# A gather and scatter kernel that sorts edges first: shorter last chunks, chunks of 16 tiles with one-hots on GpSimd in the first stage, and fewer VectorE operations

## The chip, the cores and the metric

The kernel runs on one core of a Trainium2 chip. The core has TensorE (PE, matrix products; its weight loads are listed apart as PEld), VectorE (DVE), ScalarE (ACT), GpSimd (POOL) and SyncE (SP), and 16 DMA engines that all queues share. The metric is the device time of one execution in microseconds; lower is better. A profile is taken of one execution; its span runs from the first to the last instruction.

## The reference

There are N = 10000 nodes with features x of shape (N, 64, 4), and E = 640000 edges. Each edge has a source, a destination, a vector Y of 4 and a feature vector of 4. All is float32, and source and destination are drawn at random.

```python
R = silu(edge_feat @ w_rad)                    # (E, C)
xs = x[src]                                    # (E, C, M)
tp = einsum('eci,ef,ifo->eco', xs, Y, cg)      # (E, C, M)
msg = R[:, :, None] * tp
agg = segment_sum(msg.reshape(-1, C * M), dst, N).reshape(N, C, M)
return einsum('ncm,cd->ndm', agg, w_mix)
```

## The kernel before

The kernel never adds into memory edge by edge. It sorts the edges by destination, in two passes, so that the edges of 32 neighbouring nodes (a bucket) lie in one block of slots, and then sums each bucket with matrix products. Edges are handled in tiles of 128, one per partition; 5000 tiles in all. What is moved for an edge is a record of W = 9 words: source and destination packed into one word, Y, and the edge features.

**Parts.** `SPLIT` cuts the edges into three parts of 1488, 1776 and 1736 tiles. Pass 1 (`pass1`) distributes the records of a part over NG = 20 groups (array `grp` in DRAM); pass 2 (`pass2`) distributes a group's records over its 15 or 16 buckets (array `bkt`). A segment is one group of one part, so there are 60 segments. `messages` then works through the buckets in units of 5 tiles (first part) or 6 (the others): it gathers rows of x, one indirect DMA on GpSimd per tile (`gather`, line 808), multiplies them by the radial factors (`products`, line 852), builds S from one-hots and Y (`spots`, lines 842 and 845) and sums G on TensorE (`sums`, line 863). The sums of the first two parts go to DRAM and are added to in the next; the third part ends with the mix by `w_mix` and the store of the output (`mix`, line 911).

**Stages.** `run` has three. The lead-in is pass 1 of the first part alone. There only SP's order is written out by hand, and the other engines' is made by a scheduler. The second stage, `groups`, writes out the order on TensorE, VectorE and ScalarE: it interleaves the generators of `messages`, pass 2 of the next segment, and pass 1 of the next part, each by a count of steps that are due. The orders of GpSimd and SP are the scheduler's. The third stage, `overflow`, is a loop on the device over records that found no room, 128 slots an iteration; each iteration is a chain of a load, a gather of x, a gather of the output, products and a scatter to the output (lines 1062 to 1142).

**One chunk of a pass** (`route`). A chunk is up to T = 24 tiles of one part or segment (`even` splits evenly: 62, 74 and 73 chunks in pass 1, 4 in each segment of pass 2). `tables` has counted before, for up to `NC` chunks at a time, how many edges of each tile go to each of the B targets; `digits` makes the 0/1 array `D` that it counts. For a chunk, `places` and `placed` compute for every edge its position through two products and a copy on ScalarE; `slots` (lines 482 to 485: a maximum and three small operations on VectorE) turns it into a row (0 to 127) and a slot. `spread` builds X: a mask (line 496) and a product of mask and record (line 499), for 6 tiles at a time, as wide as the widest of the six needs. `onehots` builds `oh`, the one-hot of the rows: with 12 tiles in a piece (half a chunk), 6 are made by VectorE (line 512) and `act` = 6 by ScalarE (lines 517 and 518). `move` multiplies `oh` by X into PSUM (line 528), `evict` copies the result to `rt`, and `store` (line 546) writes its rows, each S slots long, with one indirect DMA on GpSimd. Steps are spread over the counter k of `route`: a chunk is loaded 6 steps ahead, its positions come 5 and 4 ahead, slots 3 ahead.

**Overflow of a chunk.** A target has a fixed room (`cap`). If a chunk's end for a target lies beyond it, the whole block of that chunk and target (R rows of S slots) goes to the overflow area instead (`over` and `inc`, lines 420 to 424; `ko`, lines 445 to 447), and the count in `kov`, in blocks, sets the number of iterations in `overflow` (line 1044). R is 6 in pass 1 and 8 in pass 2, S is 39 and 35.

The array `self.dv` in PSUM holds constants that VectorE reads (`v128`) and two scratch areas (`eq` of `spots`, `vmsk` of `spread`), so that an operation reads at most one operand from SBUF.

Of the kernel before, what the change touches and what calls it, by code (L numbers as in the profile page):

```python
# [60 lines left out]
class Pass:  # L61
# [18 lines left out]
    def spans(self, a, z):  # L80

        return [(t, min(t + 6, z), max(self.w[t:min(t + 6, z)])) for t in range(a, z, 6)]
# [19 lines left out]
class Kernel:  # L102
    def __init__(self, ctx, tc, x, src, dst, Y, ef, w_rad, cg, w_mix, out):
# [40 lines left out]
        self.p1 = Pass(T, NG, P // NG, [n / N for n in self.gn], 1.5, 5e-9)  # L144
# [6 lines left out]
        p, R = self.p1, self.p1.R  # L151
        self.gcap = [max(g) * P // R for g in self.gt]
        p.stride = [-(-(c + p.S) // 64) * 64 for c in self.gcap]
        p.base = [0]
        for st in p.stride:
            p.base.append(p.base[-1] + NG * R * st)
        p.ovf = p.base[-1]
        p.blocks = sum(len(even(z - a, T)) for a, z in self.part) * NG
# [3 lines left out]
        p.blocks = sum(len(even(t, T)) for t in sum(self.gt, [])) * MB  # L162
        for p in (self.p1, self.p2):
            p.slots = p.ovf + p.blocks * p.R * p.S + 2 * P
        self.p1.key, self.p2.key = "grp", "bkt"
        self.xw = max(sum((z - a) * w for a, z, w in p.spans(c, d)) * W for p in (self.p1, self.p2)
                      for m in range(T // 2, T + 1) for c, d in p.pieces(m))

        self.p1.NC, self.p2.NC = 12, max(len(even(t, T)) for t in sum(self.gt, []))
        self.p1.dst = self.dr.tile([self.p1.slots, W], F, name="grp")  # L170
        self.p2.dst = self.dr.tile([self.p2.slots, W], F, name="bkt")
# [3 lines left out]
        self.held, self.wanted, self.pos = None, False, None  # L175

# [6 lines left out]

    def consts(self):
        nc, c = self.nc, self.cst

        def iota(name, pat, base=0, cm=0, at=c):
            t = at.tile([P] + [n for _, n in pat], F, name=name)
            nc.gpsimd.iota(t, pattern=pat, base=base, channel_multiplier=cm,
                           allow_small_or_imprecise_dtypes=True)  # L190
            return t
# [11 lines left out]
        self.eq = self.dv[:, P:P + UT * NB].rearrange("p (t n) -> p t n", n=NB)  # L203
        self.vmsk = self.dv[:, P + UT * NB:]
# [9 lines left out]
        for p in (self.p1, self.p2):  # L214

            k, T, B = p.key, p.T, p.B
            p.cols = c.tile([64, B * (T + 1)], F, name="cols" + k)
            nc.vector.memset(p.cols, 0.0)
            nc.vector.memset(p.cols.rearrange("p (b t) -> p b t", b=B)[:, :, 0:1], RESET)
            p.low = c.tile([64, B * (T + 1)], F, name="low" + k)  # L220
            nc.gpsimd.memset(p.low, 0.0)
            p.lot = c.tile([P, T], F, name="lot" + k)
            nc.gpsimd.memset(p.lot, 0.0)
            for t in range(T):
                if p.lo[t]:
                    nc.gpsimd.memset(p.low.rearrange("p (b t) -> p b t", b=B)[:, :, t:t + 1], float(p.lo[t] * p.R))
                    nc.gpsimd.memset(p.lot[:, t:t + 1], float(p.lo[t]))
            p.A = c.tile([P, P], BF, name="A" + k)
            nc.vector.tensor_scalar(p.A, self.U, float(B), None, op0=OP.mult)
            nc.vector.scalar_tensor_tensor(p.A, self.ident, BIG, p.A, op0=OP.mult, op1=OP.add)  # L230

            j = iota("j" + k, [[0, 1]], base=0, cm=1, at=self.ph)
            ji = self.ph.tile([P, 1], I32, name="ji" + k)
# [220 lines left out]
    def route(self, ps, chunk, sizes, table):  # L454
# [97 lines left out]
        for k in range(-6, NP + self.ls):  # L552
# [20 lines left out]
            if k % 2 and 0 <= k + 3 < NP:  # L573
                slots((k + 3) // 2)
# [638 lines left out]
```

## Time and profile before

| | us |
|---|---|
| median of 3 runs | 8622.01 |
| lowest and highest run | 8620.0, 8624.1 |
| the profiled execution | 8610.05 |
| its span | 8608.1 |

| stretch of the span, us | what runs |
|---|---|
| 0 to 36 | constants, first loads, first tables |
| 36 to 588 | lead-in: pass 1 of the first part |
| 588 to 738 | pass 2 of the first segment, pass 1 of the second part beside it |
| 738 to 3195 | messages of the first part, by the gathers' issue |
| 3195 to 5875 | messages of the second part |
| 5875 to 8328 | messages of the third part |
| 8328 to 8608 | last sums and stores, then the overflow loop |

Over the whole span TensorE is busy 86% of the time, VectorE 81%, GpSimd 65% and ScalarE 43%. In a table of stretches each row has start and end, length, then for each engine the busy time and the number of instructions, the granted TensorE clock as a share of full speed, the busy share of the DMA engines and GB/s. A row of waits reads: engine and line that waited, what it waited for, total us, times, longest. A row of a timeline has the start, the length, the engine, the line, the operation with its tiles and shapes, and in brackets the idle time before it. A row of groups has line, engine, operation, shape and count, then busy time and the mean of one in ns. On GpSimd, 0.30 us between two indirect DMAs appears as idle time ("issue").

### The profile page before, as it was taken

Reading aid. Unit: us, or ns where it says so; the run is one execution under the profiler, and the core shown is the slowest. Engines: PE = TensorE matmul, PEld = TensorE weight load, DVE = VectorE, ACT = ScalarE, POOL = GpSimd, SP = SyncE. Lnnn points to the kernel's source line nnn. Section 1 sums busy time; section 2 is a strip of 40 time slices with the busy share of each in tenths; the row PEclk is TensorE's granted clock in tenths of the full one; section 3 lists DMA queues with packets and bytes.
Section 4 is the critical chain, followed back from the end, with each engine's and each line's share of the span. In section 5 each row is a group of like instructions: output and inputs, shape, how many; then the busy total and the mean of one; then the engine's idle time right before and its main releaser. Section 6 shows DMA issues by size and latency. Waiting matters only on the chain. (4 is left out here: it accounts for less than half of the span.)

```text
span 8608.1 us, 141721 instructions
## 1 busy us (share of the span) xinstructions
PE 7366.7 (86%) x49106; PEld 6316.5 (73%) x49106; DVE 6967.2 (81%) x13381; ACT 3692.0 (43%) x10312; POOL 5578.9 (65%) x5982
## 2 busy tenths in 40 slices
PE   7878989889989888999999899887988998889862
PEld 6767777777877777777777778766777777777651
DVE  8988888898988789999999999776776677667533
ACT  6765555555555444444444445332332233223200
POOL 0104766666666767777676777777777777777751
PEclk9988989899999899999989999988989999899875
DMA  7113444344444444545454554554444444444430
GB/s 271 46 30 86 136 117 118 112 122 119 122 119 120 134 121 139 142 139 145 135 140 136 143 144 135 156 145 138 134 134 133 136 134 133 134 135 131 132 91 11
DMA packets 677211, 1086.50 MB, mean 126 GB/s; under 512 B 255927, under 2 KB 481651, under 8 KB 670232
## 3 DMA queue, kind: packets, MB, share of 16 engines
q0 software_dynamic: 282384, 774.50, 31.7%
q1 hardware_dynamic: 392968, 295.28, 11.9%
q8 instruction: 389, 6.37, 0.3%
q10 hardware_dynamic: 1152, 7.74, 0.2%
q14 instruction: 318, 2.61, 0.1%
HBM read 857.68 MB, written 222.06 MB: 125 GB/s over the span
## 5 line engine op out<-in xcount | busy, mean ns | idle before, releaser
L808 POOL DMA_INDIRECT xg<-in_x_dram,sidx x5321 | 5072.6, 953 | 1976.3 <-issue 1406.1
L528 PE MATMUL pr<-X,oh 128*128 128x135 f32 (+14 forms) x20530 | 2754.9, 294 | 342.3 <-DVE oh L512 247.8
L528 PEld LDWEIGHTS pr<-X,oh 128*128 128x128 f32 x20530 | 2623.4, 202 | 507.9 <-DVE oh L512 281.7
L863 PE MATMUL G<-S,xg 128*128 128x128 f32 x21284 | 2933.0, 301 | 11.3 <-DVE Gs L892 5.2
L863 PEld LDWEIGHTS G<-S,xg 128*128 128x128 f32 x21284 | 2831.5, 216 | 71.1 <-DVE Gs L892 33.8
L852 DVE TENSOR_TENSOR xg<-xg,pre 128x1536 f32<-128x1536 f32 (+1 forms) x939 | 1558.4, 1660 | 864.1 <-DMA xg<-in_x_dram,sidx 717.6
L499 DVE TENSOR_TENSOR X<-dv,Wt 128x918 f32<-128x918 f32 (+12 forms) x1796 | 1620.5, 902 | 163.8 <-PE pr L528 82.2
L517 ACT ACTIVATE sq<-i,row 128x128 f32<-128x128 f32 x5388 | 1663.2, 390 | 47.8 <-DVE row L485 39.9
L834 ACT ACTIVATE pre<-pre 128x384 f32<-128x384 f32 (+1 forms) x939 | 429.8, 458 | 2172.4 <-PE pre L831 2102.3
L845 DVE TENSOR_TENSOR S<-dv,pay 128x768 f32<-128x768 f32 (+1 forms) x939 | 857.5, 913 | 53.6 <-PE G L863 9.4
L831 PE MATMUL pre<-wr,sT 54*128 54x384 f32 (+1 forms) x1878 | 836.7, 526 | 22.6 <-ACT sT L826 22.5
L518 ACT ACTIVATE oh<-sq,ones 128x768 f32<-128x768 f32 x898 | 838.4, 934 | 27.5 <-issue 1.7
L512 DVE TENSOR_TENSOR oh<-dv,row 128x768 f32<-128x768 f32 (+3 forms) x898 | 780.3, 873 | 0.2
L821 PEld LDWEIGHTS pre<-ident,pay 128*54 128x54 f32 (+1 forms) x939 | 108.8, 116 | 859.7 <-DVE xg L852 676.2
L821 PE MATMUL pre<-ident,pay 128*54 128x128 f32 (+1 forms) x939 | 293.5, 313 | 511.7 <-DVE xg L852 491.6
L546 POOL DMA_INDIRECT grp<-rt,idx x209 | 213.0, 1019 | 678.4 <-ACT rt L537 477.7
L826 ACT ACTIVATE sT<-pre 54x128 f32<-54x128 f32 (+1 forms) x939 | 246.5, 262 | 818.4 <-PE pre L821 816.1
L496 DVE TENSOR_TENSOR dv<-dv,slot 128x102 f32<-128x102 f32 (+12 forms) x1796 | 445.9, 248 | 40.3
L476 ACT ACTIVATE pc<-pp 128x480 f32<-128x480 f32 (+6 forms) x449 | 226.2, 504 | 410.5 <-DVE pos L482 282.5
L831 PEld LDWEIGHTS pre<-wr,sT 54*128 54x128 f32 (+1 forms) x1878 | 282.7, 188 | 151.8 <-issue 42.6
L842 DVE TENSOR_TENSOR dv<-dv,dlc 128x192 f32<-128x192 f32 (+1 forms) x939 | 331.2, 353 | 18.1
L911 PE MATMUL po<-wf,Gs 128*128 128x256 f32 (+1 forms) x1280 | 306.8, 394 | 38.5 <-DVE over L420 31.5
(210 smaller groups left out, 4098.7 us busy)
## 6 DMA issues: line engine op xcount, KB each, us to landing
xg<-in_x_dram,sidx POOLq DMA_INDIRECT x5321
sums<-Gp SPq DMA_DIRECT2D x626, 128.0 KB
old<-sums SPq DMA_DIRECT2D x626, 128.0 KB
bkt<-z SPq DMA_DIRECT2D x26, 1024.0 KB
grp<-z SPq DMA_DIRECT2D x16, 1024.0 KB
pay<-bkt SPq DMA_DIRECT2D x208, 54.0 KB
ys<-in_Y_dram SPq DMA_DIRECT2D x96, 96.0 KB
es<-in_edge_feat_dram SPq DMA_DIRECT2D x96, 96.0 KB
```

The lines of the kernel that those rows point to most:

```text
L496: nc.vector.tensor_tensor(msk, self.v128[:, :w].unsqueeze(1).to_broadcast([P, m, w]), slot[:, t:e].unsqueeze(2).to_broadcast([P, m, w]), o ...
L499: nc.vector.tensor_tensor(x, msk.unsqueeze(3).to_broadcast([P, m, w, W]), CH[c][1][:, t:e, :].unsqueeze(2).to_broadcast([P, m, w, W]), op= ...
L512: nc.vector.tensor_tensor(oh[:, :v, :], self.v128.unsqueeze(1).to_broadcast([P, v, P]), row[:, a:a + v].unsqueeze(2).to_broadcast([P, v, P ...
L517: nc.scalar.activation(sq[:, u - v, :], self.i128, AF.Square, bias=row[:, a + u:a + u + 1], scale=-1.0)
L518: nc.scalar.activation(oh[:, v:m, :], sq[:, :m - v, :], AF.Relu, bias=self.ones[:, 0:1], scale=-2.0)
L528: nc.tensor.matmul(PR[c][:, ps.lo[t] * W:ps.hi[t] * W], oh[:, u, :], Xs[u], start=(t == 0), stop=(t == sizes[c] - 1), skip_group_check=True)
L808: nc.gpsimd.indirect_dma_start(out=xg[:, t, :], out_offset=None, in_=self.x, in_offset=bass.IndirectOffsetOnAxis(ap=si[:, u:u + 1], axis=0))
L831: nc.tensor.matmul(R, ST_.pop(k)[:ut * W], self.wr[:ut * W, :ut * 64], start=True, stop=True)
L834: nc.scalar.activation(RT[k], RT[k], AF.Silu)
L845: nc.vector.tensor_tensor(S[:, :ut], self.eq[:, :ut].unsqueeze(3).to_broadcast([P, ut, NB, 4]), pb[:, :, 1:5].unsqueeze(2).to_broadcast([P ...
L852: nc.vector.tensor_tensor(V, V, R.unsqueeze(3).to_broadcast([P, ut, 64, 4]), op=OP.mult)
L863: nc.tensor.matmul(G[:, h].rearrange("p n f -> p (n f)"), V[:, t, 32 * h:32 * h + 32, :].rearrange("p c i -> p (c i)"), S[:, t].rearrange( ...
```

## The change

*Last chunk.* `sizes2` gives the segments of the third part a fifth chunk of 6 tiles; the other four share the rest (22, 22, 22, 21 and 6 where it was 24, 23, 23, 23). Rows of that chunk have S = 12 slots. The overflow counts slots now, not blocks: `over` is multiplied by a column `sc` of slots per block (one more VectorE operation in `tables`), and a row `ov` replaces the factor R x S.

*Lead-in.* Pass 1 of the first part has an own `Pass` with T = 16 (93 chunks, S = 28, pieces of 8 tiles) and tables for up to 18 chunks at a time. With `spare` set, which it is in the lead-in alone, all one-hots beyond `act` = 3 are single operations on GpSimd, one for each tile of 128 x 128: 930 in all. `rt` has 20 buffers for 16, and stores come 10 steps after, not 8.

*Mask and X.* `spread` makes one mask and one X for a whole piece, with the width of the piece's widest tile.

*Slots.* The maximum stays one for each chunk; the three operations after it are done for two chunks at once. For this, chunks are loaded 8 steps ahead, positions come 7 and 6 ahead, and slots 5 ahead.

*Digits.* `two` holds each digit twice in bf16, and the compare reads `ib` (bf16, SBUF) and `two` (bf16, SBUF) in place of `v128` (float32, PSUM) and the integer digits; one operation covers 38 tiles (pass 1) or 48 (pass 2), not 24.

```diff
+    def width(self, a, z):
+        return max(self.w[a:z])
...
+        early, late = some(16), some(T)
+        self.p1 = [early] + [late] * (len(SPLIT) - 1)
...
+    def sizes2(self, k, g):
+        n, T, end = self.gt[k][g], self.p2.T, 6 if k == len(SPLIT) - 1 else 0
+        return even(n - end, T) + [end] * (end > 0)
...
     def digits(self, ps, D, dig, nt):
-        for o in range(0, nt, 24):
-            m = min(24, nt - o)
-            self.nc.vector.tensor_tensor(D[:, o:o + m, :], self.v128[:, :ps.B].unsqueeze(1).to_broadcast([P, m, ps.B]),
-                                         dig[:, o:o + m].unsqueeze(2).to_broadcast([P, m, ps.B]), op=OP.is_equal)
+        nc, B, q = self.nc, ps.B, 768 // ps.B // 2 * 2
+        two = self.ph.tile([P, dig.shape[1], 2], BF, name="two", tag="two" + ps.key, bufs=1)
+        nc.vector.tensor_copy(two[:, :nt], dig[:, :nt].unsqueeze(2).to_broadcast([P, nt, 2]))
+        yield
+        for o in range(0, nt, q):
+            m = min(q, nt - o)
+            nc.vector.tensor_tensor(
+                D[:, o:o + m, :].rearrange("p t (b e) -> p t b e", e=2),
+                self.ib[:, :B].rearrange("p (b e) -> p b e", e=2).unsqueeze(1).to_broadcast([P, m, B // 2, 2]),
+                two[:, o:o + m].unsqueeze(2).to_broadcast([P, m, B // 2, 2]), op=OP.is_equal)
             yield
...
-        nc.vector.tensor_tensor(over[:N], e[:N], cap[:N], op=OP.is_gt)
-        nc.vector.tensor_tensor_scan(inc[:N], self.ones[:N, :B], over[:N], 0.0, op0=OP.mult, op1=OP.add)
+        nc.vector.tensor_tensor(over[:N, :B], e[:N], cap[:N], op=OP.is_gt)
+        nc.vector.tensor_scalar(over[:N, B:], over[:N, :B], sc[:N], None, op0=OP.mult)
+        nc.vector.tensor_tensor_scan(inc[:N], self.ones[:N, :B], over[:N, B:], 0.0, op0=OP.mult, op1=OP.add)
...
-        nc.vector.tensor_scalar(ko, Kp, float(R * ps.S), ps.ovj[:Q], op0=OP.mult, op1=OP.add)
+        nc.vector.tensor_tensor(ko, Kp, ov[:Q, :N], op=OP.add)
...
         def slots(c):
+            m, a = sizes[c], c % 2
...
+            nc.vector.tensor_reduce(pos[:, a, :m], PP.pop(c).rearrange("p (t b) -> p t b", b=B), axis=AX.X, op=OP.max)
+            if a == 0 and c + 1 < N:
+                return
...
         def spread(k):
-            for t, e, w in ps.spans(a, z):
-                m = e - t
...
+            m, w = z - a, ps.width(a, z)
+            msk = self.vmsk[:, :m * w].rearrange("p (t s) -> p t s", s=w)
+            nc.vector.tensor_tensor(msk, self.v128[:, :w].unsqueeze(1).to_broadcast([P, m, w]),
+                                    slot[:, a:z].unsqueeze(2).to_broadcast([P, m, w]), op=OP.is_equal)
...
+            nc.vector.tensor_tensor(X, msk.unsqueeze(3).to_broadcast([P, m, w, W]),
+                                    CH[c][1][:, a:z, :].unsqueeze(2).to_broadcast([P, m, w, W]), op=OP.mult)
...
         def onehots(k):
-            if v:
+            if self.spare:
+                for u in range(v):
+                    nc.gpsimd.tensor_scalar(oh[:, u, :], self.i128, row[:, a + u:a + u + 1], None, op0=OP.is_equal)
+            elif v:
...
-        for k in range(-6, NP + self.ls):
+        for k in range(-8, NP + self.ls):
...
-            self.rt_bufs, self.ls, self.act = 16, 8, 6
+            self.rt_bufs, self.ls, self.act, self.spare = 20, 10, 3, True
...
-                first = self.pass1(0, 4)
+                first = self.pass1(0, 6)
...
-            self.rt_bufs, self.ls, self.act = 3, 4, 6
+            self.rt_bufs, self.ls, self.act, self.spare = 3, 4, 6, False
```

More of the change, by code (lines that the diff above doesn't have):

```diff
@@ L184, in consts @@
     def consts(self):
         nc, c = self.nc, self.cst
[L187 to L191, printed above, removed]
+        iota = self.iota
         self.zr = c.tile([16, 8 * W], F, name="zr")
@@ L450, in tables @@
         nc.vector.tensor_tensor(idx[:Q, :N], ko, ii, op=OP.add)
-        self.tab[ps.key] = (sb, idx)
+        self.tab[ps.key] = (sb, idx, runs)
         yield
```

245 lines of the change are left out of this document (132 added, 113 removed).

## The prediction

> **What bounds the kernel now.** I read the table of time slices first, then cut the span where the work changes (first gather of x, last gather of each part of `SPLIT`, end of the messages) and read the busy time of each engine in each stretch.
>
> ```profile
> core 0: us, PE busy (x) PEld busy (x) DVE busy (x) ACT busy (x) POOL busy (x), PEclk, DMA share, GB/s
> 36.00:588.00 552.00, 470.43 (x3244) 406.99 (x3244) 523.14 (x1090) 408.66 (x1107) 61.43 (x62) 0.96 0.32 114
> 588.00:738.00 150.00, 102.97 (x604) 87.21 (x604) 118.00 (x299) 77.67 (x213) 9.93 (x11) 0.72 0.13 34
> 738.00:3195.00 2457.00, 2177.12 (x15013) 1897.40 (x15011) 2134.86 (x4248) 1305.91 (x3727) 1655.02 (x1723) 0.90 0.43 122
> 3195.00:5875.00 2680.00, 2397.38 (x16497) 2065.08 (x16498) 2397.41 (x4365) 1174.82 (x3234) 1940.41 (x2026) 0.92 0.51 142
> 5875.00:8328.00 2453.00, 2126.88 (x13488) 1802.22 (x13487) 1670.90 (x2828) 702.57 (x1950) 1858.44 (x1950) 0.90 0.47 133
> 8352.00:8608.00 256.00, 72.35 (x184) 44.74 (x184) 97.34 (x436) 13.26 (x56) 41.94 (x42) 0.50 0.05 11
> ```
>
> Five stretches, three limits. The lead-in (36 to 588 us) is VectorE's: 523 of 552 us busy, with GpSimd nearly idle. The messages of the third part (5875 to 8328) are GpSimd's. Its waits there are all one kind:
>
> ```profile
> POOL xg L808 <- issue: 512.1, 1681, 0.3
> POOL bkt L546 <- issue: 21.0, 69, 0.3
> ...
> PE pr L528 <- DVE oh L512: 83.7, 40, 5.4
> PE pre L821 <- DVE xg L852: 81.4, 54, 4.1
> ```
>
> No wait of POOL in that stretch is above 0.3 us, so 1950 indirect DMAs in 2453 us, 1.258 us each, is its full rate, though it shows as 76% busy. By that rate the messages of the first part need 1723 x 1.258 = 2168 of 2457 us and those of the second 2026 x 1.258 = 2549 of 2680: POOL has 289 and 131 us to spare there. VectorE is 87% and 89% busy in them, TensorE 89% each at a granted clock near 0.9, and the longest waits of TensorE (last two lines above, first part) are for VectorE. So these two are set mostly by VectorE, with GpSimd close behind. The last 256 us are the overflow loop (lines 1062 to 1142), one latency chain with every engine mostly idle.
>
> **The change part by part.**
>
> *The overflow loop.* A chunk's block that would pass a bucket's end goes whole to the overflow area, in R x S slots: 8 x 35 = 280 now. The loop takes 128 slots an iteration.
>
> ```profile
> 8403.99 1.01 POOL L1140 DMA_INDIRECT out_dram<-ocur,odi  x1 [8.19 <-DVE ocur L1139]
> ...
> 8580.02 1.01 POOL L1140 DMA_INDIRECT out_dram<-ocur,odi  x1 [8.24 <-DVE ocur L1139]
> ```
>
> In GpSimd's timeline these two end the 3rd and 13th iteration of 14: 176.03 / 10 = 17.60 us each. Applying the kernel's slot rules to the reference's edges with seed 0 gives 6 overflowing blocks, all last chunks of the third part: 6 x 280 = 1680 slots, 13.1, so 14 iterations, as the profile has. Afterwards the last chunk is 6 tiles, S = 12, 96 slots; the same rules give again 6 blocks, 576 slots, 4.5, so 5 iterations. 9 x 17.60 = **-158 us**. Nothing hides this loop, so nothing hides its loss. The lower count of slots is exact if the six blocks stay six; a seventh or eighth would cost at most one iteration.
>
> *The fifth chunk.* Each of 20 segments of the third part gets one more store on POOL, the engine that sets that stretch.
>
> ```profile
> 4309.16 0.95 POOL L808 DMA_INDIRECT xg<-in_x_dram,sidx  x1 [0.30 <-issue]
> 4310.41 1.51 POOL L808 DMA_INDIRECT xg<-in_x_dram,sidx  x1 [0.30 <-DVE Gp L892]
> 4332.28 1.02 POOL L546 DMA_INDIRECT grp<-rt,idx  x1 [0.30 <-issue]
> 4333.61 0.96 POOL L808 DMA_INDIRECT xg<-in_x_dram,sidx  x1 [0.30 <-issue]
> 4309.98 1.18 DVE L395 TENSOR_TENSOR_SCAN sums<-colsgrp,lowgrp 64x500 f32<-64x500 f32 x1
> ```
>
> A store holds the queue for 4333.61 - 4332.28 = 1.33 us: 20 x 1.33 = **+27 us**, whatever the length of its rows. The extra positions, masks and products of these chunks fall on engines with over 10% idle here; with that cover gone they would be some 2 us a chunk, by the fixed parts below.
>
> *Digits.* The compare that makes `D` now reads `ib` and `two`, both in SBUF. The last line above is a VectorE operation with two SBUF inputs; the gather beside it took 1.51 instead of 0.95 us. About 226 such compares run during the messages, 40 of them in the third part, each shorter than that scan. Bounds: nothing, or 0.56 us on each: 40 x 0.56 = 22 us where POOL is the limit. I take 0.2 us: **+8 us**. The Trainium skill, GPSIMD Engine Reference, section 1, states that GpSimd's SBUF interfaces are shared with VectorE and contend with VectorE instructions that have two SBUF inputs; the pair of rows agrees, and by that rule alone the sum would be 14 us higher.
>
> *Fewer VectorE operations, second and third pass over the edges.* VectorE's timeline (start, length) has one 24-tile chunk of pass 1, and digits:
>
> ```profile
> 4321.93 0.27 DVE L496 TENSOR_TENSOR dv<-dv,slot 128x102 f32<-128x102 f32 x1
> 4322.23 1.11 DVE L499 TENSOR_TENSOR X<-dv,Wt 128x918 f32<-128x918 f32 x1
> 4323.38 0.28 DVE L496 TENSOR_TENSOR dv<-dv,slot 128x114 f32<-128x114 f32 x1
> 4323.70 1.23 DVE L499 TENSOR_TENSOR X<-dv,Wt 128x1026 f32<-128x1026 f32 x1
> ...
> 4332.15 0.78 DVE L499 TENSOR_TENSOR X<-dv,Wt 128x594 f32<-128x594 f32 x1
> ...
> 4328.38 0.18 DVE L483 TENSOR_SCALAR ci<-pos 128x24 int32<-128x24 f32 x1
> ...
> 4328.79 0.22 DVE L441 TENSOR_SCALAR ci<-fo,jbgrp 120x5 int32<-120x5 f32 x1
> 42.00 5.17 DVE L366 TENSOR_TENSOR D<-dv,da 128x480 bf16<-128x480 f32 x9
> 4317.57 0.40 DVE L411 CAST sb<-at 64x480 bf16<-64x480 f32 x1
> ```
>
> From 594 to 1026 elements X grows by 0.45 us: 1.04 ns an element and 0.16 fixed; a mask has the same fixed part. Four pairs become two, which drops 4 fixed parts, 0.64, and some 0.1 of waits between mask and X (0.03 to 0.04 each, from start to start); but one width for 12 tiles makes X 12 x (14 + 19) x 9 = 3564 elements instead of 3294, and masks 396 instead of 366: +0.31. Net -0.4 us. The three slot operations (start of ci to the next kind, 0.41 us) come once for two chunks: -0.17. Digits cost 5.17 / 9 = 0.57 a chunk; the new compare lies between the same rate per element (no gain) and the rate of the bf16 cast in the last line, 0.40 for 480, so 0.2 less with the copy `two`; I take the cast, which like it writes bf16 from SBUF. That is 0.8 us a chunk, bounds 0.5 and 1.0 (a 20-tile chunk of pass 2 drops as many fixed parts for 216 more elements and comes to the same). The first two parts hold 147 + 160 chunks: 307 x 0.8 = 245 us off VectorE, bounds 150 and 310. The Trainium skill, VectorE: DVE Perf Modes, section on the perf-mode tier table, puts a two-input operation on bf16 in SBUF at twice the fp32 rate; the cast row is its nearest relative here, and without it the 245 would be 185.
>
> Not all of it reaches the end: POOL can follow by 289 + 131 us at most, TensorE stands at 89%, though its clock of 0.9 should rise as its gaps close. I let two thirds arrive: **-165 us**, bounds -40 and -400.
>
> *The lead-in.* 62 chunks of 24 tiles become 93 of 16; 5 of 8 one-hots go to POOL, 3 to ScalarE. From TensorE's timeline, then from the groups by form (busy, mean ns of one):
>
> ```profile
> 334.40 2.91 PE L528 MATMUL pr<-X,oh 128*128 128x45 f32 x24
> 338.28 3.38 PE L528 MATMUL pr<-X,oh 128*128 128x126 f32 x24 [0.96 <-DVE oh L512]
> 342.23 2.92 PE L528 MATMUL pr<-X,oh 128*128 128x45 f32 x24
> ...
> L512 DVE TENSOR_TENSOR oh<-dv,row 128x768 f32<-128x768 f32 x103 | 97.7, 948 | 0.0
> L517 ACT ACTIVATE sq<-i,row 128x128 f32<-128x128 f32 x600 | 185.8, 389 | 40.4 <-DVE row L485 35.4 <-DVE Wt L649 2.9 <-DVE ovr L424 1.6
> ...
> L337 POOL IOTA prm<- 128x128 f32 x1 | 0.4, 390 | 0.0
> L189 POOL IOTA dif<- 128x128 f32 x1 | 0.2, 248 | 0.0
> L1175 POOL MEMSET zw<- 128x128 f32 x1 | 0.2, 209 | 2.1 <-issue 2.1
> ```
>
> Now a chunk takes 342.23 - 334.40 = 7.83 us of VectorE's time, 62 x 7.83 = 485, and 67 us of the 552 go to table batches and the start. A new chunk on VectorE: X of 864 and 1152 elements 1.06 + 1.36, masks 0.58, the maximum 0.45, slots 0.2, copy 0.1, digits 0.3: 4.05 us. On TensorE: 16 tiles at 2.91 / 12 = 0.243 us, 3.9, places 0.4 (341.66 to 342.23 now, for two thirds of the columns) and counts 0.2: 4.5. ScalarE: 6 squares at 185.8 / 600 = 0.31, 2 half-size one-hots, 3 copies, an eviction: 3.8. POOL: ten compares of 128x128 and a store of 1.33. The trace has no such compare; its nearest rows of that size run from 0.21 (memset) over 0.25 and 0.39 (iota) to 0.39 (the square on ScalarE). At 0.32 POOL needs 10 x 0.32 + 1.33 = 4.5 us, level with TensorE. The Trainium skill, GPSIMD Engine Reference, section 8, warns that VectorE is about twice as fast at elementwise work; 948 / 6 = 158 ns a tile now, doubled, is the same 0.32 as an estimate. Taking 4.6 us a chunk: 93 x 4.6 + 67 = 495, **-57 us**; at 0.21 TensorE's 4.5 still holds, -66; at 0.39 it is 5.23 us, +1.
>
> *Setup and transition.* Three sets of constants instead of two, and positions two steps earlier, cost a few us in 0 to 36 and one chunk of pass 1 earlier in 588 to 738; that chunk is then not done in the messages. Zero.
>
> Sum: -158 + 27 + 8 - 165 - 57 = -345 us, against the profiled execution's 8610: 8265. The median of the three runs is 12 us above it; **8270**, its own range 8180 to 8350.
>
> **The rivals.**
>
> *Relief without progress.* TensorE, at 89%, or the chain from gather over transpose to product becomes the limit in the first two parts, and VectorE merely idles more. For it: waits that VectorE itself has there leave it only 87 to 89% busy. Against: TensorE's longest waits name VectorE. Price: 165 us back, **8435**.
>
> *POOL's whole spare time is taken.* Gaps close, the clock rises, the gathers run back to back from the first: -400 instead of -165, **8035**. Against: three engines near 90% interlock.
>
> *GpSimd's compare is dear.* It becomes the bound of the lead-in, beyond 0.32 us, and outgrows what it replaces from 0.39. At 0.5 us a chunk takes 6.33: 93 x 6.33 + 67 = 656, +104, so **8430**. The whole turns slower than before where the lead-in pays back the other 288 us: 552 + 288 = 840, 8.3 us a chunk, 0.70 us a compare. At the time of POOL's indirect DMA, 0.95 us, a chunk is 10.8, the lead-in 1074: +522, **8850**. For it: POOL has no such operation in the trace; against: every other row of 128x128 lies below 0.4.
>
> *The tail stays.* If the counting of slots kept 14 iterations, **8430**.
>
> **How the numbers follow.** Forecast 0.60; relief without progress 0.14; POOL's spare time taken 0.07; compare dear but the whole still faster 0.09; so dear that it is slower 0.05; tail unchanged 0.05. Low end 8120, between forecast and second rival; high end 8435, which takes in the first rival, the compare at 0.5 and the unchanged tail, and leaves out the dearer compares. About 0.2% (17 us) is what a measurement tells from no change. Faster 0.94, same 0.01, slower 0.05.
>
> **What would show it.** Five rows of the overflow write, 17.6 us apart; third part's messages some 30 us longer at 1.26 us per indirect DMA with 1970 of them; VectorE under 85% busy in the first two parts and POOL's waits above 0.3 us down by more than 100 us; in the lead-in a mean of POOL's compare at or under 0.35 us, and TensorE over 90% busy. Wrong if POOL is over 90% busy in the lead-in, if first-part and second-part messages keep their 2457 and 2680 us, or if iterations stay above 6.

## The result, and the profile after

| | before | after |
|---|---|---|
| median, us | 8621.01 (4 runs, 8614.35 to 8624.1) | 12255.01 (4 runs, 12245.22 to 12260.18) |
| ratio to before | | 1.4215, 95% interval 1.419 to 1.424 |
| the profiled execution; its span | 8610.05; 8608.1 | 12260.18; 12258.4 |

The forecast was 8270 us, within 8120 to 8435. The changed kernel takes 12255. The table of stretches of the changed kernel is cut at the same events as that of before: last store of the lead-in, first gather, last gather of each part, end. The columns are those of the first fence of the prediction.

```profile
36.00:814.00 778.00, 577.24 (x3335) 503.89 (x3334) 385.15 (x852) 374.67 (x1115) 652.58 (x1023) 0.76 0.24 83
814.00:953.00 139.00, 100.80 (x639) 83.44 (x640) 115.33 (x265) 79.77 (x218) 10.28 (x12) 0.75 0.16 38
953.00:3264.00 2311.00, 2122.91 (x14951) 1845.10 (x14950) 2007.48 (x3375) 1305.40 (x3717) 1662.57 (x1722) 0.92 0.46 129
3264.00:5872.00 2608.00, 2352.17 (x16535) 2025.04 (x16534) 2288.91 (x3589) 1189.29 (x3262) 1953.60 (x2029) 0.93 0.52 146
5872.00:8352.00 2480.00, 2131.30 (x13528) 1796.32 (x13529) 1615.40 (x2593) 757.27 (x2141) 1879.86 (x1968) 0.90 0.47 132
8352.00:12258.00 3906.00, 1140.98 (x2907) 708.81 (x2906) 1526.54 (x6808) 208.46 (x877) 660.07 (x661) 0.50 0.05 12
```

| stretch | before | after | difference | forecast |
|---|---|---|---|---|
| lead-in, from 36 us | 552 | 778 | +226 | -57 |
| to the first gather | 150 | 139 | -11 | 0 |
| messages of the first part | 2457 | 2311 | -146 | -165 in both |
| messages of the second part | 2680 | 2608 | -72 | |
| messages of the third part | 2453 | 2480 | +27 | +27 + 8 |
| last gather to the end | 280 | 3906 | +3626 | -158 |

The first five rows add up to +24 us. All the rest, 3626 of 3650 us, is the last row. Two views of the changed kernel's tail: GpSimd's group of the writes to the output, one in each iteration (count, busy time, mean in ns, idle time before), and from its timeline the first three and the last of these writes.

```profile
L1189 POOL DMA_INDIRECT out_dram<-ocur,odi x219 | 222.7, 1017 | 1843.7 <-DVE ocur L1188 1843.7
```

```profile
8392.02 1.03 POOL L1189 DMA_INDIRECT out_dram<-ocur,odi  x1 [8.33 <-DVE ocur L1188]
...
8416.65 1.02 POOL L1189 DMA_INDIRECT out_dram<-ocur,odi  x1 [8.41 <-DVE ocur L1188]
8434.61 1.02 POOL L1189 DMA_INDIRECT out_dram<-ocur,odi  x1 [8.66 <-DVE ocur L1188]
...
12248.33 1.02 POOL L1189 DMA_INDIRECT out_dram<-ocur,odi  x1 [8.39 <-DVE ocur L1188]
```

219 iterations for 14, where the forecast had 5. The pitch, (12248.33 - 8416.65) / 217 = 17.66 us, is what it was; only the count is wrong. 205 more iterations at 17.66 are 3620 us.

The lead-in has turned from VectorE's stretch into GpSimd's: VectorE busy 385 of 778 us (523 of 552 before), GpSimd 653. In its timeline ten compares take 5.84 us, and in the list of all of them the median is 0.594 us each, where the forecast took 0.32:

```profile
700.00 5.84 POOL L558 TENSOR_SCALAR oh<-i,row 128x128 f32<-128x128 f32 x10
706.04 1.06 POOL L595 DMA_INDIRECT grp<-rt,idx  x1 [0.20 <-issue]
707.15 5.84 POOL L558 TENSOR_SCALAR oh<-i,row 128x128 f32<-128x128 f32 x10
713.19 1.06 POOL L595 DMA_INDIRECT grp<-rt,idx  x1 [0.20 <-issue]
```

```profile
L558 POOL TENSOR_SCALAR oh<-i,row x930: 592/594/1234, 35.9 to 809.6; 128x128 f32<-128x128 f32 x186
```

(The last row has the shortest, median and longest in ns, then the first and the last start.) One chunk here is ten compares and a store, 707.15 - 700.00 = 7.15 us, with no gap on GpSimd but the 0.2 us ahead of a store: it is the bound, and 93 x 7.15 = 665 us. The other 113 of the 778 us are in part waits of GpSimd itself, as its groups from 150 to 780 us show (at the end of each line the idle time before, and what ended most of it): 47 us for TensorE, and 34 us at stores that wait for the clearing of `grp`.

```profile
L558 POOL TENSOR_SCALAR oh<-i,row 128x128 f32<-128x128 f32 x737 | 437.3, 607 | 53.0 <-PE pr L576 47.0 <-DVE row L531 0.9 <-ACT sq L565 0.7
L595 POOL DMA_INDIRECT grp<-rt,idx x84 | 90.1, 1072 | 50.6 <-DMA grp<-z 33.8 <-issue 13.9 <-DMA grp<-rt,idx 1.0
```

In the messages, VectorE's work shrank as forecast, from 2134.86 + 2397.41 to 2007.48 + 2288.91 us: 236 us less, where 245 were expected; and 146 + 72 = 218 us of them arrived at the end of the stretches.

The runs that follow fell on several chips, each with its own runs of the kernel before beside it. On some the kernel before takes 8.6 ms, as here, on others 10.2 to 10.4 ms (called the slower kind below); so times go with their ratios, and stretches are compared only between chips of one kind. The lead-in and an iteration of the overflow loop take the same time on both.

### The profile page after: what moved, and what is told of

It is laid out like the page before. It is cut to its first block, busy times and chain, and to the rows that moved or that the text cites. A ratio compares the mean times of both kernels' runs of the same rounds, so it can differ in the third digit from the quotient of the medians.

```text
span 12258.4 us, 167463 instructions
## 1 busy us (share of the span) xinstructions
PE 8433.0 (69%) x51924; PEld 6966.9 (57%) x51924; DVE 7968.6 (65%) x17630; ACT 3919.6 (32%) x11344; POOL 6830.6 (56%) x7609
## 5 line engine op out<-in xcount | busy, mean ns | idle before, releaser
L576 PE MATMUL pr<-X,oh 128*128 128x81 f32 (+14 forms) x20530 | 2773.2, 295 | 316.2 <-DVE X L544 108.0
L544 DVE TENSOR_TENSOR X<-dv,Wt 128x1512 f32<-128x1512 f32 (+12 forms) x1000 | 1560.5, 1561 | 223.1 <-PE pr L576 100.9
L1189 POOL DMA_INDIRECT out_dram<-ocur,odi x219 | 222.7, 1017 | 1843.7 <-DVE ocur L1188 1843.7
L1140 PE MATMUL opd<-ident,odst 128*128 128x128 f32 x438 | 174.2, 501 | 1381.8 <-DVE odst L1121 1381.8
L1180 PE MATMUL opm<-oeq,oM 128*128 128x128 f32 x876 | 261.5, 454 | 1082.8 <-DVE oM L1176 1082.8
L566 ACT ACTIVATE oh<-sq,ones 128x768 f32<-128x768 f32 (+1 forms) x1000 | 862.1, 862 | 104.6 <-PE pr L576 70.3
L1180 PEld LDWEIGHTS opm<-oeq,oM 128*128 128x128 f32 x876 | 203.4, 323 | 1123.4 <-issue 1123.4
L1135 POOL DMA_INDIRECT oxg<-in_x_dram,osi x219 | 211.6, 966 | 990.4 <-DVE odst L1121 990.4
L1176 DVE SCALAR_TENSOR_TENSOR oM<-oV,oA,oM 128x64 f32<-128x64 f32 x2628 | 668.3, 325 | 0.0
L560 DVE TENSOR_TENSOR oh<-dv,row 128x768 f32<-128x768 f32 (+3 forms) x774 | 646.4, 840 | 0.0
```

The source lines that it names most:

```text
L544: nc.vector.tensor_tensor(X, msk.unsqueeze(3).to_broadcast([P, m, w, W]), CH[c][1][:, a:z, :].unsqueeze(2).to_broadcast([P, m, w, W]), op= ...
L560: nc.vector.tensor_tensor(oh[:, :v, :], self.v128.unsqueeze(1).to_broadcast([P, v, P]), row[:, a:a + v].unsqueeze(2).to_broadcast([P, v, P ...
L566: nc.scalar.activation(oh[:, v:m, :], sq[:, :m - v, :], AF.Relu, bias=self.ones[:, 0:1], scale=-2.0)
L576: nc.tensor.matmul(PR[c][:, ps.lo[t] * W:ps.hi[t] * W], oh[:, u, :], Xs[u], start=(t == 0), stop=(t == sizes[c] - 1), skip_group_check=True)
L1176: nc.vector.scalar_tensor_tensor(M[:, :, o], V[:, :, i], A[:, 4 * i + o:4 * i + o + 1], M[:, :, o], op0=OP.mult, op1=OP.add)
L1180: nc.tensor.matmul(pm[:, h, :], M[:, 32 * h:32 * h + 32, :].rearrange("p c o -> p (c o)"), eq, start=True, stop=True)
```

## The experiments

**Why the overflow loop runs 219 times.** The theory came from reading `tables` again. The running count of a chunk's slots is a scan that is held up at a floor, `low`, for each tile (line 432), and the chunk's end is read in the column after the last tile of the longest chunk, whatever the chunk's own length (`m` is `sizes[0]`):

```python
nc.vector.tensor_tensor_scan(sums, ps.cols, ps.low, 0.0, op0=OP.add, op1=OP.max)
...
nc.vector.tensor_copy(n[:N], sums[:N, :, m])
```

With chunks of 24 and 23 tiles this does nothing. A chunk of 6 tiles beside one of 22 has 16 columns without edges, but the floor goes on rising in them to 18 x 8 = 144 slots (17 x 8 = 136 where the longest has 21). By the slot rules and the edges of seed 0 the short chunk holds 29 to 65 edges of a bucket, 47 in the mean, and the bucket has room for 103 more in the mean: 47 fit nearly always, 136 or 144 nearly never. Counted in this way 293 of the 313 blocks go over, 28128 slots, 220 iterations; the trace has 219, so one block fewer; which one is open.

The first run mends the floor and nothing else. Rows 0 to 3 belong to the long chunks of every part and row 4 to the short one alone (rows 32 to 36 are their copies), so `low` is set to zero in rows 4 and 36 from column 6 on:

```diff
             p.last = self.lists(p, c, k + "l", jr, [p.S] * (len(m) - 1) + [p.hi[m[-1] - 1]])
...
+            keep = self.ph.tile([64, 2], F, name="keep" + k)
+            for h in range(2):
+                nc.vector.tensor_scalar(keep[:, h:h + 1], self.pid[:64], float(32 * h + len(m) - 1), None,
+                                        op0=OP.not_equal)
+            nc.vector.tensor_tensor(keep[:, 0:1], keep[:, 0:1], keep[:, 1:2], op=OP.mult)
+            cut = p.low.rearrange("p (b t) -> p b t", b=B)[:, :, m[-1]:]
+            nc.vector.tensor_scalar(cut, cut, keep[:, 0:1], None, op0=OP.mult)
```

> The changed kernel with one addition: in the constants of pass 2 the floor `low` is set to zero for the row of the short last chunk (rows 4 and 36) from column 6 on, so that its end is its count and not the floor of a chunk of 22 tiles. Theory A (the floor of later columns lifts the end of the short chunk beyond the bucket's room): 5 iterations of the overflow loop for 219, so 12255 - 214 x 17.6 = 8489 us, and everything ahead of the loop stays as it is. Rival B (the new count in slots is wrong) and rival C (the fifth chunk really starts too near the end of the room): the floor does not matter, still about 219 iterations and 12255 us.

The second leaves the short chunk out, and the third makes it 12 tiles long (12 in place of the 0 below), both with the floor as it was:

```diff
-        n, T, end = self.gt[k][g], self.p2.T, 6 if k == len(SPLIT) - 1 else 0
+        n, T, end = self.gt[k][g], self.p2.T, 0 if k == len(SPLIT) - 1 else 0
```

> The changed kernel without the short last chunk (segments of the third part in four even chunks again), all else as changed, the count in slots included. Theory A: all rows end within one tile of the longest, the floor lifts nothing, 14 iterations as before the change: 12255 - 205 x 17.6 - 27 for twenty stores that are gone = 8620 us. Rival B (the count in slots is wrong): another number of iterations than 14. Rival C: 14 iterations too, 8620 us.

> The changed kernel with a last chunk of 12 tiles for 6 (longest chunk 20 or 21 for 22), floor left as it is. Theory A: 12 tiles hold about twice the edges of 6 while the floor they are lifted to is lower, so fewer blocks go over: the slot rules with the floor taken to the longest chunk's end, applied to the edges of seed 0, give 67 blocks x 160 slots = 10720, 84 iterations, 12255 - 135 x 17.6 = 9879 us. Rival C (whatever chunk comes fifth goes over): about 292 blocks x 160 slots = 365 iterations, 12255 + 146 x 17.6 = 14825 us.

All three fell on a chip where the kernel before takes 10348 us. One line of GpSimd's groups in the tail of each, in the same order:

```profile
L1197 POOL DMA_INDIRECT out_dram<-ocur,odi x5 | 5.1, 1022 | 42.1 <-DVE ocur L1196 42.1
```

```profile
L1189 POOL DMA_INDIRECT out_dram<-ocur,odi x13 | 13.3, 1020 | 107.2 <-DVE ocur L1188 107.2
```

```profile
L1189 POOL DMA_INDIRECT out_dram<-ocur,odi x84 | 85.7, 1020 | 698.6 <-DVE ocur L1188 698.6
```

5, 13 and 84 iterations. The floor mended gives the 5 that the forecast had; the chunk of 12 tiles gives the 84 that the floor's rule gives, far from the 365 of "whatever comes fifth goes over". The second was expected to give 14 and gave 13, which the expectation had set down as a sign of a wrong count. But the changed kernel gives the last of the four chunks its own number of slots, 34 for 35 (`p.hi` for 23 tiles), so six blocks are 6 x 272 = 1632 slots, 12.75, 13 iterations. With 5, 13 and 84 all as the slots give them, the count in slots is right. Times: 10344 us (ratio 0.9993, 0.9976 to 1.001) with the floor mended, 10386 us (1.0033, 1.0016 to 1.0051) without the short chunk, 11729 us (one run) with 12 tiles. The last is 1385 us above the first, for 79 more iterations: 17.5 us each.

The kernel of the first run was run twice more, to measure it on a chip of the other kind.

> The changed kernel with the floor mended and nothing else, run again on another chip than the first time. Theory A (the floor is the whole cause of the long tail): everything to the last gather as in the changed kernel (8352 us), 5 iterations, 127 us from the last gather to the end: 8480 us, 1.5% below the kernel before. Rival (something else of the change holds up the end too): 8600 us or more.

> The changed kernel with the floor mended and nothing else. On a chip that takes some 8610 us for the kernel before: 5 iterations and 8480 us by theory A (the floor is the whole cause of the long tail), 0.985 of the time before; 8600 us or more by the rival (something else of the change holds up the end too). Where the kernel before takes over 10000 us, a ratio of 0.998 as in the two runs so far.

Both fell on the slower kind again: 10208 us for 10233 (0.9975, 0.9959 to 0.9991) and 10343 for 10357 (0.9985, 0.9968 to 1.0002), 5 iterations each. The 8480 us of theory A were therefore not measured as such. What was measured on the faster kind are seven kernels with the floor mended and other changes in the lead-in or in the passes (below), all with 5 iterations and 123 to 128 us from the last gather to the end.

**The lead-in.** The fourth run adds to the mended floor the lead-in as before:

```diff
-        early, late = some(16), some(T)
+        early, late = some(T), some(T)
...
-            self.rt_bufs, self.ls, self.act, self.spare = 20, 10, 3, True
+            self.rt_bufs, self.ls, self.act, self.spare = 16, 8, 6, False
...
-                first = self.pass1(0, 6)
+                first = self.pass1(0, 4)
```

> The kernel of the first run (floor mended) with the lead-in as before the change: chunks of 24 tiles, six one-hots of twelve in one VectorE operation, six on ScalarE, tables for up to 12 chunks. Theory: the dear GpSimd one-hots alone cost the lead-in its 226 us, so 8489 - 226 = 8263 us or less, the last store of the lead-in at 588 us or earlier, since digits, mask and slots still save VectorE some 0.8 us in each of 62 chunks (50 us, 8213). Rival: the lead-in is longer because chunks are loaded and placed two steps earlier or because two SBUF operands slow things down, and not because of GpSimd: then it stays well above 588 us, and the time near 8489.

> The kernel with the floor mended and the lead-in as before the change, run again beside the next three, of which it is the base. Theory: first gather near 675 us as in its first run, messages as in the changed kernel (7399 us from the first gather to the last) and 127 us from there to the end with 5 iterations: 675 + 7399 + 127 = 8201 us, which would be 0.951 of the time before. Rival (the shorter lead-in is paid back in the messages): 8300 us or more.

The first time, on the slower kind of chip: 10052 us for 10348, 0.9716 (0.9692 to 0.974), first gather at 674.8 us. The second time, on a chip where the kernel before takes 8611: **8189 us, 0.952 (0.9507 to 0.9533)**, faster than both kernels of the comparison. Its stretches of lead-in and messages (the first gather is at 674.4 us, the end at 8181):

```profile
36.00:535.00 499.00, 454.47 (x3248) 398.63 (x3247) 483.58 (x752) 413.49 (x1117) 61.68 (x62) 0.97 0.35 126
```

```profile
674.00:2967.00 2293.00, 2092.42 (x14950) 1817.99 (x14950) 2008.31 (x3378) 1305.30 (x3716) 1655.08 (x1721) 0.93 0.46 130
2967.00:5581.00 2614.00, 2367.85 (x16536) 2041.72 (x16536) 2289.86 (x3589) 1189.86 (x3264) 1947.85 (x2030) 0.92 0.52 146
5581.00:8056.00 2475.00, 2139.04 (x13537) 1804.57 (x13538) 1616.97 (x2593) 757.43 (x2141) 1875.19 (x1969) 0.90 0.47 132
8056.00:8181.00 125.00, 35.84 (x117) 24.58 (x115) 39.73 (x174) 5.13 (x21) 17.75 (x19) 0.54 0.05 12
```

The lead-in is 499 us, 53 below before (fewer VectorE operations, as forecast for the messages), and nothing of that is paid back in the messages. Three more runs ask which half of the new lead-in costs its time, the chunks of 16 tiles or the one-hots on GpSimd, and what a compare is made of. A profile of the kernel before was taken beside them.

```diff
-            self.rt_bufs, self.ls, self.act, self.spare = 20, 10, 3, True
+            self.rt_bufs, self.ls, self.act, self.spare = 20, 10, 5, True
...
+            self.rt_bufs, self.ls, self.act, self.spare = 20, 10, 3, False
...
-                    nc.gpsimd.tensor_scalar(oh[:, u, :], self.i128, row[:, a + u:a + u + 1], None, op0=OP.is_equal)
+                    for q in (0, 64):
+                        nc.gpsimd.tensor_scalar(oh[:, u, q:q + 64], self.i128[:, q:q + 64], row[:, a + u:a + u + 1],
+                                                None, op0=OP.is_equal)
```

The first two lines are the run with five one-hots of eight on ScalarE, the third the run with five on VectorE, the last three the run with half compares.

> The kernel before, profiled again beside the others, so that its stretches can be compared with theirs on one chip. Theory (the chip of the first four runs grants TensorE a lower clock and holds up its instructions in the messages, whatever the kernel): where the time is near 10348 us, lead-in and overflow loop are as in the first profile (587.8 us to the last store of the lead-in, 14 iterations of 17.6 us) and only the messages are longer. Rival (the chip is slower throughout): lead-in and loop are longer by the same fifth.

> The kernel with the floor mended, lead-in in chunks of 16 tiles, but 5 one-hots of 8 on ScalarE and 3 on GpSimd (3 and 5 before). Theory (GpSimd's 0.593 us a compare and 1.33 a store are the bound, 7.3 us a chunk): GpSimd falls to 6 x 0.593 + 1.33 = 4.9 us a chunk, ScalarE rises to some 5.4, so 93 x 1.9 = 177 us off the lead-in, first gather near 780 us for 956. Rival (the chunk's latency through four engines, or ScalarE, sets the pace): less than 60 us off.

> The kernel with the floor mended, lead-in in chunks of 16 tiles, with the five one-hots that GpSimd made now in one VectorE operation of 128x640. Theory (GpSimd is the bound, 16-tile chunks are not): VectorE has 4.05 + 2 x 5 x 0.158 = 5.7 us a chunk and becomes the bound, 93 x 1.6 = 150 us off the lead-in, first gather near 800 us for 956. Rival (16-tile chunks cost the lead-in its time through their number, 93 for 62): first gather stays above 900 us.

> The kernel with the floor mended, each GpSimd compare of 128x128 cut in two of 128x64. It measures what the 0.593 us are made of. Theory: mostly per element, 0.32 us for a half, two of them 0.64: the lead-in grows by 93 x 10 x 0.05 = 45 us. Rival: mostly a fixed part, 0.5 us for a half, two of them 1.0: the lead-in grows by 93 x 10 x 0.4 = 370 us.

These fell on a chip where the kernel before takes 8613 us. One run each: before 8606, ScalarE 8394, VectorE 8216, half compares 8671. The profile of before is that of the first comparison again (first gather at 738.9 us for 738.2, end 8603.9 for 8608.1), so it tells nothing of the slower chips. The lead-in of the other three, from 36 us to its last store:

```profile
36.00:731.00 695.00, 537.81 (x3337) 471.94 (x3336) 389.11 (x855) 507.79 (x1488) 433.09 (x651) 0.82 0.27 93
```

```profile
36.00:565.00 529.00, 469.44 (x3337) 404.71 (x3336) 492.94 (x1041) 374.41 (x1115) 92.58 (x93) 0.95 0.35 122
```

```profile
36.00:1009.00 973.00, 681.57 (x3337) 575.93 (x3336) 378.24 (x855) 375.57 (x1115) 881.29 (x1952) 0.67 0.19 66
```

Chunks of 16 tiles with the one-hots on VectorE take 529 us, 23 less than before; the same chunks with the one-hots on GpSimd 778. So it is GpSimd's compares, 249 us, and not the number of chunks; against the lead-in in chunks of 24 tiles (499 us) the chunks of 16 cost 30 us. With fewer of them, 3 of 8, the lead-in takes 695: 83 us less, where the engine sums said 177. No engine is busy in it for more than 538 of 695 us; the longest waits from 150 to 700 us are those of a ring:

```profile
DVE X L552 <- PE pr L584: 164.6, 106, 4.2
POOL oh L566 <- PE pr L584: 130.4, 94, 10.5
ACT rt L594 <- PE pr L584: 100.5, 63, 5.3
PEld pr L584 <- POOL oh L566: 87.7, 108, 1.9
```

GpSimd waits for TensorE to give a one-hot buffer back (`oh` has three), and TensorE waits for GpSimd's next one-hots. A sum for each engine by itself is a lower bound there. The half compares:

```profile
L567 POOL TENSOR_SCALAR oh<-i,row x1860: 430/431/1775, 36.5 to 1004.8; 128x64 f32<-128x64 f32 x186
```

0.431 us for 64 elements a partition and 0.594 for 128: 0.163 / 64 = 2.55 ns an element, and, if time grows evenly with the elements, a fixed part of 0.431 - 0.163 = 0.268 us. Neither expectation (0.32 and 0.5) was right.

**Which of the fewer operations pay.** Base is the kernel of 8189 us. One run gives two of VectorE's six one-hots in a piece of the lead-in to GpSimd; one has the digits' compare as before; one has mask and X in operations of six tiles.

```diff
             if self.spare:
+                g = min(self.spare, v)          # 2 in the lead-in
+                if v > g:
+                    nc.vector.tensor_tensor(oh[:, g:v, :], self.v128.unsqueeze(1).to_broadcast([P, v - g, P]),
+                                            row[:, a + g:a + v].unsqueeze(2).to_broadcast([P, v - g, P]),
+                                            op=OP.is_equal)
-                for u in range(v):
+                for u in range(g):
...
+            for b in range(a, z, 6):
+                e = min(b + 6, z)
+                m, w = e - b, ps.width(b, e)
```

(The digits' part is the change's diff of `digits` turned round; of the six-tile run the diff shows the loop in `spread`, with mask and X inside it.)

> The base, but in the lead-in's pieces of 12 tiles two of the six one-hots of VectorE go to GpSimd. Theory: GpSimd has 4 x 0.593 + 1.33 = 3.7 us a chunk to do and does not bound, VectorE loses 4 x 0.158 = 0.63 us a chunk, TensorE follows at some 6.5 us: 62 x 0.3 to 0.6 = 20 to 40 us off, 8170 us. Rival (TensorE is the bound already, 440 of 484 us busy): no change.

> The base with the digits' compare as before the change (PSUM constant, one SBUF operand, 24 tiles at a time). Theory: a 24-tile chunk pays 0.65 us for 0.35 + 0.05 again, a 20-tile chunk 0.55 for 0.28 + 0.05, about 0.23 us x 307 chunks = 71 us back on VectorE, nearly all of which reaches the end as in the change itself (236 us of VectorE became 218 us): 65 us slower than the base. Rival (two SBUF operands cost GpSimd's gathers as much as VectorE gains): no difference, or faster.

> The base with mask and X again in operations of six tiles, each as wide as it needs. Theory: 0.4 us a chunk come back on VectorE, 307 x 0.4 = 123 us in the first two parts and 62 x 0.4 = 25 us in the lead-in: some 120 to 145 us slower than the base. Rival (the wider X gives back what the fewer operations save): under 30 us slower.

| kernel | median, us | ratio to before, 95% interval | first gather | first, second, third part |
|---|---|---|---|---|
| base | 8189 | 0.952 (0.9507 to 0.9533) | 674 | 2293, 2614, 2475 |
| two one-hots on GpSimd | 8164 | 0.9481 (0.9468 to 0.9494) | 651 | 2295, 2611, 2477 |
| digits as before | 8267 | 0.96 (0.9587 to 0.9614) | 705 | 2364, 2611, 2469 |
| mask and X of six tiles | 8308 | 0.9652 (0.9638 to 0.9665) | 701 | 2346, 2666, 2475 |

The first came out as expected and the other two nearly so: -25 us (for 20 to 40), +78 (for 65) and +119 (for 120 to 145). Where GpSimd has only 4 compares of a chunk it does not bound and the lead-in gains 25 us; this is the fastest kernel of the study. The digits' two forms, from VectorE's groups in the first two parts, in the run with the old form and in the changed kernel:

```profile
L404 DVE TENSOR_TENSOR D<-dv,da 128x480 bf16<-128x480 f32 x127 | 79.4, 649 | 0.8
```

```profile
L400 DVE TENSOR_TENSOR D<-ib,two 128x760 bf16<-128x760 bf16 x69 | 35.9, 548 | 0.1
```

649 / 480 = 1.35 ns an element against 548 / 760 = 0.72. The Trainium skill, VectorE: DVE Perf Modes, section on the perf-mode tier table, puts a two-input operation on bf16 in SBUF at twice the rate of one with an operand in PSUM; the rows, 1.9 times apart with their fixed parts in them, come near it. The gain of the bf16 form lies in the lead-in and up to the first gather (31 us between the two profiles) and in the first part (71); in the second and third part the old form is 3 and 6 us faster, which is little for one profile each. X of six tiles and X of twelve, from the same view of the kernel before and of the changed kernel:

```profile
L499 DVE TENSOR_TENSOR X<-dv,Wt 128x918 f32<-128x918 f32 x140 | 156.1, 1115 | 38.3 <-PE pr L528 31.0
L499 DVE TENSOR_TENSOR X<-dv,Wt 128x1026 f32<-128x1026 f32 x124 | 152.0, 1226 | 4.3
```

```profile
L544 DVE TENSOR_TENSOR X<-dv,Wt 128x2052 f32<-128x2052 f32 x124 | 284.7, 2296 | 25.1 <-PE pr L576 17.9 <-DVE dv L540 0.5
L544 DVE TENSOR_TENSOR X<-dv,Wt 128x1512 f32<-128x1512 f32 x139 | 240.8, 1733 | 14.0 <-PE pr L576 5.6
```

(2296 - 1733) / 540 = 1.04 ns an element, as the forecast had it for the small ones: twice the length costs twice the elements and one fixed part.

**The short last chunk where the floor is mended.** Base without it, twice:

> The base (8189 us, 0.952 of the time before) without the short last chunk: four even chunks in the segments of the third part, 13 iterations of the overflow loop for 5. Theory (fifth chunk: 20 stores of 1.3 us, hidden otherwise): +8 x 17.6 - 27 = +114 us, 8303 us, 0.964. Rival (the fifth chunk holds up the messages as on the slow chip, by 105 us): +36 us, 8225 us, 0.955.

> The base (0.952 of the time before) without the short last chunk, 13 iterations for 5. Where the kernel before takes some 8610 us: +114 us, 0.965, by the theory that the fifth chunk costs 27 us of stores; +36 us, 0.956, if it costs 105 us as on the chips that hold up the messages.

Both fell on the slower kind: 9992 us for 10233 (0.9773, 0.9732 to 0.9814) and 10127 for 10357 (0.9782, 0.9754 to 0.981), with 13 iterations. On such a chip the base has 0.9716 (0.9692 to 0.974, which just meets the first of these intervals), so the short chunk gains 0.6 to 0.7% there, some 60 to 70 us: 8 iterations saved (141 us) against a third part of 3038 us for 2953 on a chip of the same speed. On the faster kind the gain of the whole was not measured; from its parts there, the iterations and a third part of 2475 to 2480 us for 2453, it would be an estimated 115 us.

## Why the prediction was wrong

*Overflow loop, -158.* This is the step that failed: "Applying the kernel's slot rules to the reference's edges ... the same rules give again 6 blocks, 576 slots". The rules were applied with each chunk's count ending at its own last tile. The kernel's scan ends at the last tile of the longest chunk and raises the count to the floor on the way. For chunks within one tile of each other the two agree, and so they agreed on the kernel before (14 iterations), which was no test of the difference. The run with the floor mended gives the 5 iterations, and the one of 12 tiles the 84 that the floor gives; 214 iterations too many, at 17.66 us, are 3779 of the 3985 us by which the forecast was missed. The rival "the tail stays" looked at the right place, but only as a gain that is lost, with 0.05. The forecast did say that its count holds "if the six blocks stay six", but it priced only a seventh or eighth, and no rival let the number of blocks grow further, in the one stretch that nothing hides.

*Lead-in, -57.* The mechanism was one of the rivals (GpSimd's compare becomes the bound, 0.14 with both forms), the size was mis-set in the sum: 0.594 us a compare for 0.32, above all rows from which the bound was drawn (0.21 to 0.39), since these rows are other operations. By the sum's own formula 93 x (10 x 0.594 + 1.33) + 67 = 743 us; measured 778. The estimate beside it from the Trainium skill, GPSIMD Engine Reference, section 8 (VectorE about twice as fast), gave the same 0.32, since it doubled a tile's share, 158 ns, of an operation on six tiles, and so left out most of the fixed 0.268 us. VectorE pays its own fixed part once for six tiles, GpSimd one for each tile. Two rows of the kernel before, from VectorE's groups in the first two parts, give that part for the same compare:

```profile
L512 DVE TENSOR_TENSOR oh<-dv,row 128x768 f32<-128x768 f32 x386 | 364.4, 949 | 0.1
L512 DVE TENSOR_TENSOR oh<-dv,row 128x512 f32<-128x512 f32 x105 | 71.6, 682 | 0.0
```

(949 - 682) / 256 = 1.04 ns an element and 0.15 us fixed, so one tile alone would take VectorE an estimated 0.28 us. Twice that is 0.56, near the 0.594 measured.

*Fewer VectorE operations, -165.* Right in kind and nearly in size: 236 us off VectorE for 245, and 218 us at the end, 92% and not two thirds. The rival "relief without progress" falls. Undone one at a time, the digits give 68 us of the first two parts back and mask and X 105 (from the table: 4975 and 5012 us for 4907); the remaining 57 us against the kernel before were not tested alone (the paired slot operations, and loading and placing chunks two steps earlier). GpSimd's waits for TensorE in the first part went from 224 to 104 us:

```profile
POOL xg L857 <- issue: 410.4, 1346, 0.3
...
POOL xg L857 <- PE G L912: 104.1, 49, 9.0
```

The row of the kernel before, in the same stretch:

```profile
POOL xg L808 <- PE G L863: 224.4, 75, 9.8
```

VectorE's share stayed at 87 and 88% and did not fall under 85%, since the stretches shrank with it. The granted clock rose from 0.90 and 0.92 to 0.92 and 0.93.

*Fifth chunk and digits' contention, +27 and +8.* The third part is 27 us longer, for 35. It has 1969 indirect DMAs by its two groups on GpSimd, 19 more, at 2480 / 1969 = 1.26 us each as before, so the store's price and the bound hold. The 8 us are not shown: in this part's timeline, with 32 compares of the digits for 40, the gathers that overlap one took 0.97 us in the mean (31 of them) and the others 0.95, some 0.4 us in all, and the 6 us that the old form gives back come from one profile.

*The sum.* With 5 iterations the changed kernel would come to some 12258 - 214 x 17.66 = 8479 us of span: faster than before by 1.5%, and some 210 us above the forecast. That is an estimate, as this kernel alone was not measured on the faster kind. Of it the lead-in is 283 us too long, from which 53 us go that the first two parts gained beyond the forecast.

## What to carry to other kernels

Where one item of a batch is made much shorter than the others, look for every reduction, scan or read that runs to the batch's longest item, and for what it does in the empty columns. A count that reproduces the old kernel does not test a rule that the old kernel never brings into play. Before work goes to another engine for its spare time, measure its instruction there: a price from other operations of the same size, or a tile's share of one operation on six tiles, misses the fixed part, and many small instructions pay it each time.

## What the runs showed of the hardware that was not expected

Chips differ by a fifth on this kernel, and nearly all of it lies in the messages. The third part with the mended floor, on a chip where the kernel before takes 10348 us, and GpSimd's and TensorE's waits in it:

```profile
7175.00:10212.00 3037.00, 2320.38 (x13532) 1938.67 (x13530) 1628.42 (x2596) 751.67 (x2141) 1873.10 (x1968) 0.82 0.38 108
```

```profile
POOL xg L865 <- remote: 232.5, 100, 3.5
POOL xg L865 <- PE G L920: 211.2, 67, 10.0
...
PEld G L920 <- issue: 127.8, 118, 6.9
```

3037 us for 2480, at a granted clock of 0.82 for 0.90, with the same instructions; VectorE, ScalarE and GpSimd are busy for the same time as on the other kind. GpSimd, which on the faster kind has no wait above 0.3 us in this part, now waits for TensorE and for something that the profile names only as remote, and TensorE's weight loads wait with nothing shown that holds them. The first and second part grow too, from 2311 and 2608 to 2884 and 3335 us. The lead-in (first gather at 956 us for 953) and an iteration of the loop (17.5 us) are as elsewhere; from the last gather to the end it is 150 us for 123 to 128. Why the messages take longer on these chips was not found. It changes what an edit is worth: with the fifth chunk the third part takes 85 us longer there (3038 for 2953), and 27 us longer in the first comparison, other edits included.
